# A fused attention and squared-ReLU kernel: row statistics, one v load and one k and q load at other places

## The chip, the cores and the metric

The kernel runs on one core of one Trainium2 chip. A core has five engines that run side by side, each through its own instructions in order: PE (TensorE, matrix products), DVE (VectorE), ACT (ScalarE), POOL (GpSimd) and SP (SyncE, which here only issues transfers). ACT issues some transfers too. All transfers are carried by 16 DMA engines. The metric is the device time of one execution in microseconds; the median of three runs of the kernel before is 487.42 us (486.31 to 488.24).

## The reference

The input x is 2048 rows of 512. It is normalised by row, and the result xn feeds two branches:

```python
x = A_x
xn = _layernorm(x, axis=-1)
s = _A_ref(xn, A_wqkv, A_wo)
g = _silu(_B_ref(xn, B_w1, B_b1, B_w2, B_b2))
return x + s * g
```

Branch A is attention with 32 heads of 16: each row looks at itself and at 7 rows before it, at distances of 2, 4, ... 14. So q, k and v come from one product with wqkv (512 x 1536), logits and sums over eight rows follow, and then a product with wo. Branch B is a layer of 1792 with the square of a ReLU: `h = xn @ w1 + b1`, `r = max(h, 0)`, `r * r @ w2 + b2`. All is in float32.

## The kernel before

**Tiles and stages.** The rows of x are 16 tiles of 128, and two tiles, a and a + 1, are a pair. In the first stage (up to about 140 us) each pair gets its row statistics, is normalised and transposed, and goes through the products for q, k and v. In the second stage PE runs, for four chunks of 512 rows, branch B ("up" into ph, "down" into pb) and the product with wo (pw), without a hole; meanwhile DVE works through the attention in eight units of 256 rows. Each float32 operand is split into a high and a low part, and a product takes three passes (high x high, high x low, low x high).

**The way of a tile in the first stage.** From tile 8 on, `spread(t)` computes the statistics: two ACT instructions that read all of x and keep only a sum (their output is a tile called waste), and then three small POOL operations. `norm(t)` writes the normalised tile into xn on ACT. `shuffle(t)`, for both tiles of a pair, has SP send xn to xb in four pieces, and then has it load the x tiles two pairs ahead. DVE transposes xb into PSUM (pxT); ACT copies it to xt, the high part. For a pair "of seven" (4 to 14) the products are done on sums and differences of quarters of x: DVE forms them (Sf), ACT makes their high parts and DVE their low parts. Both parts are called S, in two halves: S_0 feeds the products T1 and T2, S_1 feeds T3 and K1.

**The products of a pair of seven**, in PE's order, for pairs 6 to 12: Q0, T1, V0 and one on vsum; T2, vsum; Q1, V1; T3, vsum; K1, V1; T4, vsum. Those called pm are 512 wide, those called pv 256 wide, six matmuls each. In the profile Q0, Q1 and T4 read `pm<-wq,xt`, and T1, T2, T3 and K1 read `pm<-wq,S`. Three PSUM tiles hold them, and ACT must copy one out before PE adds to it again:
- Q0 leaves a sum that ACT copies to a second tile (`pm<-pm`, line 805) before T2 goes on in the first (line 815).
- T3's result is copied to q's staging tile (`stg<-pm`, in `sixth`, line 830) before T4 goes on in the same PSUM tile (line 864).

The staging tiles stg have four buffers, three of which a pair uses, so q's staging tile of a pair is the v staging tile of the pair before, and ACT can write it only when that one's store to sv has landed. `store_qkv` has SP store a pair's k, v and q to sk, sv and sq.

**What sets the order.** Every instruction is recorded in the order in which the Python code calls it (which is why most lines of the profile read L90, the recording helper, and L103 for SP's transfers). The pairs are written out in `pair_of_seven`, which after each of its products calls `beside(a, step)`, step 0 to 5. `beside` runs what the table `plan` holds for that place; the table is filled by `at(a, step, ...)` and, for the statistics, by `slots`. `ahead` says at which places `next_w` splits the next pair of w1 and w2 slices for branch B: two ACT instructions (`w<-w1r`, `w<-w2r`) and two on POOL. Last, `beside` calls `pump`, which fills the DVE with pieces of the attention by a clock of estimated costs. The attention asks for a unit's k, q and v with `load`, which waits until the unit's rows are stored and then defers the transfer to a due time; it is issued on ACT (`load_u`), at the first `pump` after that time. The buffers of k, q and v are one each, so a load also waits for the unit before.

Of the kernel before, what the change touches and what calls it, by code (L numbers as in the profile page):

```python
# [1 line left out]

# [52 lines left out]
BEHIND, FAR, FREE, LAND, LOAD = 5000, 9000, 2000, 4500, 10500  # L55
# [3 lines left out]
def body(ctx: ExitStack, tc: tile.TileContext, x, wqkv, wo, w1, b1, w2, b2, out):  # L59
# [3 lines left out]
    clock = {"PE": 0.0, "V": 0.0}  # L63
# [153 lines left out]
    def windows(t, i0, dims):  # L217

        part = t[:, i0]
        return bass.AP(tensor=part.tensor, offset=part.offset, ap=[part.ap[0], *dims])  # L220


    done_tiles = {n: [0, {}] for n in "qkv"}
    done_units = [0]

    def load_u(what, u):
        n = BI if what == "q" else WIN
        src = dict(q=sq, k=sk, v=sv)[what]

        t = att.tile([P, n, CH], F32, name=f"{what}{u}", tag="k" if (what, u) == ("v", NU - 1) else what)  # L230
        row = src[0, u * UP:u * UP + 1, :]
        ap = bass.AP(tensor=row.tensor, offset=row.offset, ap=[[BI * CH, NB], [src.shape[1] * CH, GR], [1, n * CH]])
        A.dma_start(t.rearrange("p i c -> p (i c)"), ap)
        return t
# [5 lines left out]
    def defer(t, f):  # L240
        behind.append((t, f))
        behind.sort(key=lambda b: b[0])

    def flush(t):
        while behind and (t is None or behind[0][0] <= t):
            behind.pop(0)[1]()

    def attention():

        tiles, Ls, landing, exps = {}, {}, {}, set()

        def qk(u, s):
            i0 = 4 * s
            yield from there("k", u)
            yield from there("q", u)
            q, k, L = tiles["q", u], tiles["k", u], Ls[u]
            yield 2350
            pr = att.tile([P, W, 2 * P], F32, name=f"pr{u}_{s}", tag="pr")  # L260
            qv = q[:, i0:i0 + 4, :].rearrange("p i c -> p (i c)")[:, None, :].to_broadcast([P, W, 2 * P])
            V.tensor_mul(pr, windows(k, i0, [[DIL * CH, W], [1, 4 * CH]]), qv)
            yield 2300
            V.tensor_reduce(
                out=L[:, s * 16:(s + 1) * 16, :].rearrange("p m w -> p w m"),
                in_=pr.rearrange("p w (g d) -> p w g d", d=HD), axis=AX.X, op=OP.add)

        def there(n, u):
            while (n, u) not in tiles:
                yield None  # L270
            not_before(landing[n, u])


        def part(u, h):
            n = BI * 4 // 2
            return slice(0, 2 * n) if h is None else slice(h * n, h * n + n)

        def soft_a(u, h=None):
            yield 1500 if h is not None else 700
            m = part(u, h)  # L280
            L, n = Ls[u][:, m], m.stop - m.start
            if u == 0:
                i = slice(m.start // 4, m.stop // 4)
                lm = L.rearrange("p (i h) w -> p i h w", h=4)
                V.tensor_add(lm, lm, mask[:, i, None, :].to_broadcast([P, n // 4, 4, W]))
            mx = att.tile([P, n], F32, name=f"mx{u}_{h}", tag="mx")
            V.tensor_reduce(out=mx, in_=L, axis=AX.X, op=OP.max)
            (G if h is None else V).tensor_sub(L, L, mx[:, :, None].to_broadcast([P, n, W]))

            def exp():  # L290
                A.activation(L, L, AF.Exp, scale=0.25)
                exps.add((u, h))

            defer(clock["V"] + (BEHIND if h is not None else FAR), exp)

        def soft_b(u, h=None):
            while (u, h) not in exps:
                yield None
            yield 2100 if h is not None else 1400
            m = part(u, h)  # L300
            L, n = Ls[u][:, m], m.stop - m.start
            sm = att.tile([P, n], F32, name=f"sm{u}_{h}", tag="sm")
            V.tensor_reduce(out=sm, in_=L, axis=AX.X, op=OP.add)
            V.reciprocal(sm, sm)
            (G if h is None else V).tensor_mul(L, L, sm[:, :, None].to_broadcast([P, n, W]))

        def av(u, s):
            i0 = 4 * s
            yield from there("v", u)
            v, L = tiles["v", u], Ls[u]  # L310
            yield 2400

            pr = att.tile([P, W // 2, 2 * P, 2], F32, name=f"pv{u}_{s}", tag="pr")
            vv = windows(v, i0, [[2 * DIL * CH, W // 2], [DIL * CH, 2], [HD, 16], [1, HD]])
            l = L[:, s * 16:(s + 1) * 16, :].rearrange("p m (a e) -> p a e m", e=2)
            V.tensor_mul(pr.rearrange("p a (g d) e -> p a e g d", d=HD), vv,
                         l[:, :, :, :, None].to_broadcast([P, W // 2, 2, 16, HD]))
            yield 2300
            V.tensor_reduce(
                out=v[:, i0:i0 + 4, :].rearrange("p i c -> p (i c)"), in_=pr.rearrange("p w n e -> p n w e"),  # L320
                axis=AX.XY, op=OP.add)

        def store(u):
            v = tiles.pop(("v", u))
            row = so[0, u * UP:u * UP + 1, :]
            dst = bass.AP(tensor=row.tensor, offset=row.offset, ap=[[BI * CH, NB], [S * CH, GR], [1, BI * CH]])
            dma(dst, v[:, :BI, :].rearrange("p i c -> p (i c)"))
            done_units[0] = u + 1

        def load(u, names):  # L330
            if u == NU:
                return
            for n in names:
                while done_tiles[n][0] < 2 * (u + 1):
                    yield None

                def start(n=n):
                    tiles[n, u] = load_u(n, u)
                    landing[n, u] = clock["PE"] + LOAD

                defer(max(clock["V"] + FREE if u else 0, done_tiles[n][1][u] + LAND), start)

        yield from load(0, "kq")

        for u in range(NU + 1):
            if u < NU:
                Ls[u] = att.tile([P, BI * 4, W], F32, name=f"L{u}", tag="L", bufs=2)
                for s in range(4):
                    yield from qk(u, s)
                    if u == 0 and s % 2:  # L350
                        yield from soft_a(0, s // 2)
                    if u == 0 and s == 1:
                        while not v_ready:
                            yield None
                        yield from load(0, "v")
                if u:
                    yield from soft_a(u)
                yield from load(u + 1, "kq")
                if u == NU - 1:
                    yield from load(u, "v")  # L360
            if u == 0:
                yield from soft_b(0, 0)
            for s in range(4):
                if u > 1 or (u == 0 and s < 2) or (u == 1 and s >= 2):
                    yield from av(max(u - 1, 0), s)
            if u == 0:
                yield from soft_b(0, 1)
            if u:
                store(u - 1)
                if u < NU - 1:  # L370
                    yield from load(u, "v")
                if u < NU:
                    yield from soft_b(u)

    v_ready = []
    stream = attention()
    coming = [None]

# [345 lines left out]
    plan = {}  # L724

    def at(a, step, f, *args):
        if args[0] < NT:
            plan.setdefault((a, step), []).append((f, args))

    for a in range(2, NT, 2):  # L730
        n, t = {2: 2, 4: 1}.get(a, 0), a + 2
# [6 lines left out]
        if seven:  # L738
# [5 lines left out]
            at(a, n + 2 if n == 2 else n + 3 if n else n + 4, low_sums, t, 0)  # L744
            at(a, n + 3 if n else n + 5, low_sums, t, 1)
    slots = {6: ((2, 2), (2, 2), (2, 2), (2, 3)), 8: ((2, 4), (2, 5), (4, 0), (4, 1)),
             10: ((4, 5), (6, 0), (6, 1), (6, 2)), 12: ((6, 3), (6, 4), (6, 5), (8, 0)),
             14: ((8, 1), (8, 2), (8, 4), (8, 5))}
    for t, places in slots.items():
        for i, (a, step) in enumerate(places):  # L750
            at(a, step, norm if i > 1 else stats if t < STATS else spread, t + i % 2)
# [6 lines left out]
        at(a, step, f, n)  # L758
    for i in range(2):
        at(4, i, load_w, i)  # L760

    ahead = {(12, 3): 1, (12, 5): 1, (14, 0): 1, (14, 2): 1, (14, 4): 1}

    def beside(a, step):

        for f, args in plan.get((a, step), ()):
            f(*args)
        for n in range(ahead.get((a, step), 0)):
            next_w()
        if (a, step) == (4, 3):  # L770
            v_ready.append(True)
        pump(LATE)

    def pair(a):
# [185 lines left out]
    for c in range(NCH):  # L960
# [82 lines left out]
        else:  # L1043
# [13 lines left out]
            for j in range(2, TPC):  # L1057
                n = D // 2 if j == TPC - 1 else D
# [25 lines left out]
```

## Time and profile before

| what | value |
|---|---|
| median of three runs | 487.42 us |
| profiled execution, its own time | 487.94 us |
| its span, first to last instruction | 486.1 us |
| PE busy | 478.4 us, 98% |
| DVE busy | 422.6 us, 87% |
| ACT busy | 240.6 us, 49% |
| POOL busy | 224.8 us, 46% |
| granted TensorE clock | 1.00 throughout |

A row of the timeline has the start in us from the span's start, the time from the first start to the last end, the engine, the code line, the operation, the tile written and the tiles read, the shapes, the number of instructions, and in brackets the idle time of the engine ahead of it with what ended it. The matmuls overlap: one that is listed as 389 ns on average starts much sooner than that after the one before it. So a wait of PE shorter than this overlap is not seen as idle time, but as a longer distance between two starts. A row of a transfer in the chain has its start and how long it took to land. In the table of windows the columns are the stretch, its length, busy time and instructions of the five kinds, the granted clock, the busy share of the DMA engines and GB/s.

### The profile page before, as it was taken

To read this page: it belongs to the slowest core of one execution; us is meant where nothing else is said; L and a number is where in the kernel's file an instruction comes from. 1 tells how busy PE (TensorE), PEld (TensorE's weight loads), DVE (VectorE), ACT (ScalarE), POOL (GpSimd) and SP (SyncE) were. 2 spreads that over 40 slices of the span, in tenths; PEclk is the share of its full clock that TensorE was granted. 3 is DMA by queue.
4 is the path that set the end of the run, shared out by engine and by line. 5 is a ranking of instruction groups with operands and counts; after the bars stand their busy time and mean duration, and the time that the engine had idled before them with its cause. 6 is when DMAs were issued, how large, how long until landed. Compare 5 with 4: busy or idle time off the path is not lost.

```text
span 486.1 us, 6125 instructions
## 1 busy us (share of the span) xinstructions
PE 478.4 (98%) x2190; PEld 396.6 (82%) x2190; DVE 422.6 (87%) x352; ACT 240.6 (49%) x441; POOL 224.8 (46%) x178
## 2 busy tenths in 40 slices
PE   8999999999999999999999999999999999999996
PEld 5887888788888888888888888888888888888885
DVE  5968995989779899999999999999999999979133
ACT  5548798747475566264512444343234543423240
POOL 1358853215787599526543332443522335252210
PEclk9999999999999999999999999999999999999999
DMA  8899999997969997471618448181617734220322
GB/s 293 235 256 236 270 285 287 224 255 231 290 167 244 260 224 178 173 163 50 169 44 211 91 145 211 19 212 43 169 43 172 232 61 133 50 90 27 86 103 72
DMA packets 71002, 81.47 MB, mean 168 GB/s; under 512 B 6204, under 2 KB 55612, under 8 KB 70972
## 3 DMA queue, kind: packets, MB, share of 16 engines
q1 hardware_dynamic: 65788, 54.87, 40.8%
q10 hardware_dynamic: 5184, 26.22, 22.3%
q8 instruction: 17, 0.28, 0.2%
q14 instruction: 13, 0.11, 0.1%
HBM read 50.60 MB, written 27.32 MB: 160 GB/s over the span
## 4 chain that ended last, share of the span: by engine, by line
PE 78%; DMA 8%; DVE 6%; POOL 3%; ACT 2%; issue 2%; SPq 1%; ACTq 0%; DVEq 0%; POOLq 0%
PE pb L90 31%; PE ph L90 31%; PE pw L90 9%; DMA xb<-xn 4%; PE pq L90 4%; DMA x<-in_A_x 2%; PE pm L90 2%; DMA k<-sk 2%; POOL vsum L90 1%; DVE L L90 1%; POOL rs L90 1%; ACT stg L90 1%; ACT waste L90 1%; SPq L103 1%; DVE xt L90 1%
## 5 line engine op out<-in xcount | busy, mean ns | idle before, releaser
L90 PE MATMUL pb<-w,h 128*128 128x512 f32 x672 | 160.1, 389 | 0.0
L90 PEld LDWEIGHTS pb<-w,h 128*128 128x128 f32 x672 | 126.2, 188 | 26.1
L90 POOL TENSOR_TENSOR h<-hf,h 128x512 fp32r<-128x512 f32 x46 | 67.6, 1470 | 157.8 <-ACT hf L90 157.8
L90 PE MATMUL ph<-xU,w 128*128 128x512 f32 x504 | 120.2, 389 | 0.0
L90 ACT ACTIVATE ph<-ph,b1t 128x512 f32<-128x512 f32 x56 | 37.0, 661 | 154.6 <-PE ph L90 144.8
L90 PEld LDWEIGHTS ph<-xU,w 128*128 128x128 f32 x504 | 94.6, 188 | 19.6
L90 DVE TENSOR_TENSOR pr<-k,q 128x2048 f32<-128x2048 f32 x32 | 79.2, 2474 | 3.0 <-DMA q<-sq 2.3
L90 DVE TENSOR_TENSOR pv<-v,L 128x2048 f32<-128x2048 f32 x32 | 77.3, 2416 | 3.8 <-POOL L L90 3.1
L90 DVE TENSOR_REDUCE v<-pv 128x256 f32<-128x2048 f32 x32 | 73.0, 2280 | 0.7
L90 DVE TENSOR_REDUCE L<-pr 128x128 f32<-128x2048 f32 x32 | 73.0, 2281 | 0.7
L90 PE MATMUL pw<-wot,oT 128*128 128x512 f32 (+1 forms) x204 | 45.9, 376 | 0.0
L90 PEld LDWEIGHTS pw<-wot,oT 128*128 128x128 f32 x204 | 36.8, 188 | 7.1
L90 PE MATMUL ph<-xT,w 128*128 128x512 f32 x168 | 40.0, 389 | 0.0
L90 PE MATMUL pm<-wq,S 128*128 128x512 f32 x144 | 37.5, 395 | 1.1 <-ACT pm L90 0.5
L90 PEld LDWEIGHTS ph<-xT,w 128*128 128x128 f32 x168 | 31.5, 188 | 6.5
L90 ACT ACTIVATE h<-ph 128x512 fp32r<-128x512 f32 x56 | 33.7, 602 | 1.8
L90 POOL TENSOR_TENSOR w<-w1r,w 128x512 fp32r<-128x512 f32 x14 | 28.4, 2031 | 12.4 <-ACT w L90 9.6
L90 PEld LDWEIGHTS pm<-wq,S 128*128 128x128 f32 x144 | 25.9, 188 | 7.3 <-DVE S L90 1.9
L90 PE MATMUL pq<-wq,xT 128*128 128x512 f32 x132 | 30.8, 392 | 0.0
L90 PEld LDWEIGHTS pq<-wq,xT 128*128 128x128 f32 x132 | 24.5, 188 | 5.8 <-ACT xT L90 0.7
L90 PE MATMUL pm<-wq,xt 128*128 128x512 f32 x108 | 27.7, 393 | 0.8 <-ACT stg L90 0.8
L90 ACT ACTIVATE hf<-ph 128x512 f32<-128x512 f32 x46 | 27.3, 594 | 0.9 <-POOL h L90 0.9
(96 smaller groups left out, 533.4 us busy)
## 6 DMA issues: line engine op xcount, KB each, us to landing
k<-sk ACTq DMA_DIRECT2D x8, 960.0 KB, 7.2
v<-sv ACTq DMA_DIRECT2D x8, 960.0 KB, 7.6
sx<-xt SPq DMA_DIRECT2D x12, 512.0 KB, 5.9
xU<-sx ACTq DMA_DIRECT2D x12, 512.0 KB, 6.1
x<-in_A_x SPq DMA_DIRECT2D x16, 256.0 KB, 6.9
sk<-stg SPq DMA_DIRECT2D x8, 512.0 KB, 4.4
sq<-stg SPq DMA_DIRECT2D x8, 512.0 KB, 6.8
sv<-stg SPq DMA_DIRECT2D x8, 512.0 KB, 5.1
```

What stands on the lines that cost most here:

```text
L90: return tc.keep_in_program_order(f(*a, **k))
L103: tc.keep_in_program_order(dma(out, in_))
```

## The change

Five things are changed, all in the first stage. PE's and DVE's instructions stay the same and in the same order.

1. Statistics of tiles 10, 12 to 15: `spread` of tile 10 at pair 4's step 4 instead of 5; of tile 13 at (6, 3), with tile 12's, instead of (6, 4); of tiles 14 and 15 both at (8, 3) instead of (8, 1) and (8, 2).
2. The first unit's v was loaded when the rows were there and pair 4's step 3 was past. It is now loaded at (8, 1), from the table.
3. The second unit's k and q are no longer deferred to a due time alone: they are held until the table releases them, k at (10, 2) and q at (10, 4), behind the blocks xb of tiles 14 and 15.
4. The first w slices are split at (12, 2) instead of (12, 3), the second at (14, 0) instead of (12, 5), the third at (14, 1) instead of (14, 0); the fourth and fifth stay.
5. By that some POOL operations and one SP store trade places: POOL's adds of pair 8's k and v come ahead of the small operations of tiles 14 and 15.

```diff
+    tiles, landing, held, released = {}, {}, {}, set()
+
+    def release(n):
+        released.add(n)
+        if n in held:
+            held.pop(n)()
+
+    def start(n, u):
+        tiles[n, u] = load_u(n, u)
+        landing[n, u] = clock["PE"] + LOAD
...
             for n in names:
                 while done_tiles[n][0] < 2 * (u + 1):
                     yield None
-
-                def start(n=n):
-                    tiles[n, u] = load_u(n, u)
-                    landing[n, u] = clock["PE"] + LOAD
-
-                defer(max(clock["V"] + FREE if u else 0, done_tiles[n][1][u] + LAND), start)
+                t = max(clock["V"] + FREE if u else 0, done_tiles[n][1][u] + LAND)
+                if u == 1 and n != "v" and n not in released:
+                    held[n] = partial(start, n, u)
+                else:
+                    defer(t, partial(start, n, u))
...
-                    if u == 0 and s == 1:
-                        while not v_ready:
-                            yield None
-                        yield from load(0, "v")
...
-             10: ((4, 5), (6, 0), (6, 1), (6, 2)), 12: ((6, 3), (6, 4), (6, 5), (8, 0)),
-             14: ((8, 1), (8, 2), (8, 4), (8, 5))}
+             10: ((4, 4), (6, 0), (6, 1), (6, 2)), 12: ((6, 3), (6, 3), (6, 5), (8, 0)),
+             14: ((8, 3), (8, 3), (8, 4), (8, 5))}
...
-
-    ahead = {(12, 3): 1, (12, 5): 1, (14, 0): 1, (14, 2): 1, (14, 4): 1}
+    at(8, 1, lambda u: start("v", u), 0)
+    plan.setdefault((10, 2), []).append((release, "k"))
+    plan.setdefault((10, 4), []).append((release, "q"))
+
+    ahead = {(12, 2): 1, (14, 0): 1, (14, 1): 1, (14, 2): 1, (14, 4): 1}
...
-        if (a, step) == (4, 3):
-            v_ready.append(True)
```

ACT at the end of pair 4 and the start of pair 6, before (the two waste rows are the statistics of tile 10; stg_0 is pair 4's last copy to q, pm_1 the copy of Q0's sum that T2 of pair 6 needs):

```order
L90 ACTIVATE S_1_697<-Sf_651 128x512
L90 ACTIVATE stg_0_570<-pm_0_571 128x8x64
L90 ACTIVATE waste_713,mean_710<-x_496 128x512
L90 ACTIVATE waste_713,rs_711<-x_496,mean_710 128x512
L90 ACTIVATE pm_1_725<-pm_0_724 128x512
```

and after:

```order
L91 ACTIVATE S_1_697<-Sf_651 128x512
L91 ACTIVATE waste_704,mean_701<-x_496 128x512
L91 ACTIVATE waste_704,rs_702<-x_496,mean_701 128x512
L91 ACTIVATE stg_0_570<-pm_0_571 128x8x64
L91 ACTIVATE pm_1_725<-pm_0_724 128x512
```

The statistics of tile 10 moved ahead of pair 4's last copy to q.

ACT in pair 8, before, from the copy Sf to the high part S_0 (x_823 and x_825 are tiles 14 and 15; `stg_0<-pm_0` is T3's result on its way to q):

```order
L90 ACTIVATE Sf_976<-pxT_950 128x256
L90 ACTIVATE waste_981,mean_978<-x_823 128x512
L90 ACTIVATE waste_981,rs_979<-x_823,mean_978 128x512
L90 ACTIVATE stg_2_911<-pv_0_917 128x4x64
L90 ACTIVATE stg_0_912<-pm_1_914 128x8x64
L90 ACTIVATE stg_2_911<-pv_2_918 128x4x64
L90 ACTIVATE stg_2_911<-pv_1_916 128x4x64
L90 ACTIVATE waste_1009,mean_1006<-x_825 128x512
L90 ACTIVATE waste_1009,rs_1007<-x_825,mean_1006 128x512
L90 ACTIVATE stg_0_912<-pm_0_913 128x8x64
L90 ACTIVATE stg_2_911<-pv_0_917 128x4x64
L90 ACTIVATE S_0_1031<-Sf_976 128x512
```

and after:

```order
L91 ACTIVATE Sf_974<-pxT_948 128x256
L91 DMA v_976<-sv 128x1x1920
L91 ACTIVATE stg_2_909<-pv_0_915 128x4x64
L91 ACTIVATE stg_0_910<-pm_1_912 128x8x64
L91 ACTIVATE stg_2_909<-pv_2_916 128x4x64
L91 ACTIVATE stg_2_909<-pv_1_914 128x4x64
L91 ACTIVATE stg_0_910<-pm_0_911 128x8x64
L91 ACTIVATE stg_2_909<-pv_0_915 128x4x64
L91 ACTIVATE S_0_1013<-Sf_974 128x512
L91 ACTIVATE waste_1020,mean_1017<-x_823 128x512
L91 ACTIVATE waste_1020,rs_1018<-x_823,mean_1017 128x512
L91 ACTIVATE waste_1029,mean_1026<-x_825 128x512
```

The statistics went behind T3's copy and S_0, and the v load, which stood in pair 6 ahead of its copy of T3, came in behind Sf.

ACT in pair 12, before (w1r_593 and w2r_594 are the first slices of branch B's weights; the last row of each piece is S_1):

```order
L90 ACTIVATE stg_2_1235<-pv_1_1240 128x4x64
L90 ACTIVATE stg_0_1236<-pm_0_1237 128x8x64
L90 ACTIVATE stg_2_1235<-pv_0_1241 128x4x64
L90 ACTIVATE S_0_1336<-Sf_1294 128x512
L90 ACTIVATE w_1340<-w1r_593 128x512
L90 ACTIVATE w_1340<-w2r_594 128x512
L90 ACTIVATE S_1_1367<-Sf_1294 128x512
```

and after:

```order
L91 ACTIVATE stg_2_1235<-pv_1_1240 128x4x64
L91 ACTIVATE w_1320<-w1r_593 128x512
L91 ACTIVATE w_1320<-w2r_594 128x512
L91 ACTIVATE stg_0_1236<-pm_0_1237 128x8x64
L91 ACTIVATE stg_2_1235<-pv_0_1241 128x4x64
L91 ACTIVATE S_0_1345<-Sf_1294 128x512
L91 ACTIVATE S_1_1367<-Sf_1294 128x512
```

The two w instructions moved ahead of the copy of T3's result that T4 of pair 12 needs.

More of the change, by code (lines that the diff above doesn't have):

```diff
@@ L1 @@
 from contextlib import ExitStack
+from functools import partial
 import concourse.bass as bass
@@ L246, in flush @@
             behind.pop(0)[1]()
+    tiles, landing, held, released = {}, {}, {}, set()
[6 more added lines that the diff above has]
+        landing[n, u] = clock["PE"] + LOAD
     def attention():
-        tiles, Ls, landing, exps = {}, {}, {}, set()
+        Ls, exps = {}, set()
         def qk(u, s):
@@ L373, in attention @@
                     yield from soft_b(u)
-    v_ready = []
     stream = attention()
```

## The prediction

> **What bounds the kernel now.** I read the first part of the page, then TensorE's (PE's) rows in the timeline, then for each hole in PE the rows of the engine that released it, and last the chain and the DMA queues.
>
> ```profile
> span 486.1 us, 6125 instructions
> ...
> PE 478.4 (98%) x2190; PEld 396.6 (82%) x2190; DVE 422.6 (87%) x352; ACT 240.6 (49%) x441; POOL 224.8 (46%) x178
> ```
>
> PE is busy for 98% of the span, and the change neither adds nor removes a matmul nor changes the order of PE or DVE. So it can gain only what PE loses to waiting, and lose only by a new wait of PE. Busy time understates waiting, since rows overlap; what counts is the distance from start to start.
>
> ```profile
> 60.50 0.88 PE L90 MATMUL pv<-vsum,S 128*128 128x256 f32 x6
> 61.86 1.65 PE L90 MATMUL pm<-wq,S 128*128 128x512 f32 x6 [0.48 <-ACT pm L90]
> ...
> 84.36 0.87 PE L90 MATMUL pv<-wq,S 128*128 128x256 f32 x6
> 86.07 1.65 PE L90 MATMUL pm<-wq,xt 128*128 128x512 f32 x6 [0.84 <-ACT stg L90]
> ...
> 89.66 1.95 PE L90 MATMUL pm<-wq,S 128*128 128x512 f32 x6
> ...
> 104.76 1.52 PE L90 MATMUL pm<-wq,S 128*128 128x512 f32 x6
> 106.12 0.88 PE L90 MATMUL pv<-wq,xt 128*128 128x256 f32 x6
> ...
> 115.24 0.88 PE L90 MATMUL pv<-wq,S 128*128 128x256 f32 x6
> 115.95 1.55 PE L90 MATMUL pm<-wq,xt 128*128 128x512 f32 x6
> ...
> 119.44 0.61 PE L90 MATMUL pm<-wq,S 128*128 128x512 f32 x2
> 120.41 1.20 PE L90 MATMUL pm<-wq,S 128*128 128x512 f32 x4 [0.36 <-DVE S L90]
> 121.45 2.90 PE L90 MATMUL pq<-wq,xt 128*128 128x512 f32 x12
> ```
>
> Undisturbed, six matmuls 512 wide take 106.12 - 104.76 = 1.36 us to the next start, and six 256 wide take 115.95 - 115.24 = 0.71. By that measure four places lose time. (1) T2 of pair 6 starts at 61.86 instead of 61.21: 0.65, and its group is 1.65 long instead of 1.55: 0.75 in all. (2) T4 of pair 8 at 86.07 instead of 85.07: 1.00 + 0.10 = 1.10. (3) T1 of pair 10 is 1.95 long instead of 1.52: 0.43. (4) T1 of pair 14 takes 121.45 - 119.44 = 2.01 instead of 1.36: 0.65. Together 2.93 us, 0.6% of the span, all where the change works. This is the ceiling.
>
> **The change, part by part.** First the statistics.
>
> ```profile
> 59.27 0.60 ACT L90 ACTIVATE stg<-pm 128x512 f32<-128x512 f32 x1 [1.12 <-POOL stg L90]
> 59.76 0.62 ACT L90 ACTIVATE waste<-x 128x512 f32<-128x512 f32 x1
> ...
> 61.23 0.58 ACT L90 ACTIVATE pm<-pm 128x512 f32<-128x512 f32 x1
> ...
> 82.93 0.60 ACT L90 ACTIVATE stg<-pm 128x512 f32<-128x512 f32 x1 [0.91 <-DMA sv<-stg]
> ...
> 83.95 0.64 ACT L90 ACTIVATE waste<-x 128x512 f32<-128x512 f32 x1
> ...
> 85.44 0.58 ACT L90 ACTIVATE stg<-pm 128x512 f32<-128x512 f32 x1
> ```
>
> Hole 1: PE waits for the copy pm<-pm, which ends at 61.81; ahead of it ACT spent 59.76 to 61.23, 1.47 us, on tile 10's statistics. At (4, 4) these stand ahead of the copy at 59.27, for which ACT sat idle 1.12 us until POOL was done. So they fill that idle time, everything behind them moves up by about 1.1, and pm<-pm ends near 60.7, before PE wants it at 61.21. Gain 0.75; price nothing, because the idle 1.12 covers most of them and PE's margin of 0.5 the rest.
>
> Hole 2: T4 of pair 8 continues the sum that T3 left in the same PSUM tile and waits for its copy to q (85.44 to 86.02). That copy stood behind tile 15's statistics (83.95 to 85.44, 1.49), and these behind a copy that waited until 82.93 for pair 6's v store. Now both tiles' statistics come at (8, 3), behind the copy, which moves up by 1.49 at least, to 84.5, ahead of 85.07. Gain 1.10. Tiles 12 to 15 now have their statistics two and two ahead of the copy S_1: 1.5 us in which only DVE's second S waits.
>
> Then v.
>
> ```profile
> 78.07 1.32 DVE L90 STREAM_TRANSPOSE pxT<-xb 128x512 f32<-128x512 f32 x2 [4.83 <-DMA xb<-xn]
> ...
> 89.68 1.28 DVE L90 TENSOR_TENSOR S<-Sf,S 128x512 fp32r<-128x512 f32 x2
> ...
> 92.13 1.31 DVE L90 STREAM_TRANSPOSE pxT<-xb 128x512 f32<-128x512 f32 x2
> ...
> 102.72 1.28 DVE L90 TENSOR_TENSOR S<-Sf,S 128x512 fp32r<-128x512 f32 x2
> 106.28 1.32 DVE L90 STREAM_TRANSPOSE pxT<-xb 128x512 f32<-128x512 f32 x2 [2.27 <-DMA xb<-xn]
> ...
> 115.36 2.58 DVE L90 TENSOR_TENSOR pr<-k,q 128x2048 f32<-128x2048 f32 x1
> ...
> 119.40 2.66 DVE L90 TENSOR_TENSOR S<-Sf,S 128x512 fp32r<-128x512 f32 x2
> ```
>
> ```profile
> 66.54 0.53 ACTq L90 DMA_DIRECT2D v<-sv  x1
> ...
> 94.67 0.52 ACTq L90 DMA_DIRECT2D k<-sk  x1
> ```
>
> ```profile
> v<-sv ACTq DMA_DIRECT2D x8, 960.0 KB, 7.6
> ```
>
> ```profile
> 71.01 6.94 DMA xb<-xn
> ...
> 95.16 11.09 DMA xb<-xn
> ```
>
> ```profile
> q10 hardware_dynamic: 98, 0.75, 103.2%
> q1 hardware_dynamic: 26, 0.01, 2.3%
> ```
>
> The last two rows are the DMA queues from 69 to 72 us: ACT's queue (q10), with v, moved 0.75 MB, SP's queue (q1), with the xb blocks of tiles 10 and 11, 0.01. So v, issued at 66.54, held the blocks back (its 960 KB take 3.9 us at that rate); they landed at 71.01 + 6.94 = 77.95, and DVE, free since 78.07 - 4.83 = 73.24, waited. Without v in front they land by about 74, and the transposes start near 74 (DVE must also wait for S_1, delayed as above). That is 4 us earlier. DVE runs in order, so the S of pair 10 (89.68) comes by 86, PE wants it at 89.66 - 1.85 = 87.8: hole 3 goes, 0.43.
>
> At (8, 1) v is issued near 79 and holds SP's queue back by up to the same 3.9 us; there now stand pair 8's stores of xt and the blocks of tiles 12 and 13. DVE will want these 4 us before 92.13, at 88.1. When they land no row of before shows. Between 88.1 (v costs them nothing) and 92.1 (all 3.9), the S of pair 12, whose first half is ready at 102.72 + 0.64 = 103.4 now, comes between 99.4 and 103.4; PE will want it at 104.76 - 2.28 = 102.5. So the price lies between 0 and 0.9 us; I take 90.5 for the landing, since part of SP's queue is emptied before v starts, and charge 0.1. Behind the v issue on ACT stand four copies of pair 8; the buffer is free since the issue at 66.54 of before, so I cost that wait at nothing.
>
> Then k and q. The fourth piece of the blocks of tiles 14 and 15 took 11.09 us to 106.25, since k, issued at 94.67, and q right behind it went first. k now goes at (10, 2), behind the last piece; the transposes at 106.28 are then bound by DVE's own order, some 3 to 4 us earlier. S of pair 14 (119.40) comes near 116, PE wants it at 119.44 - 2.3 = 117.1: hole 4 goes, 0.65. DVE's first use of k and q (115.36, then near 111.5) lies some 11 us behind q's issue near 100 (an estimate from the place of S_1 of pair 12 on ACT).
>
> What is late next is pair 12:
>
> ```profile
> 112.77 0.60 ACT L90 ACTIVATE stg<-pm 128x512 f32<-128x512 f32 x1 [1.12 <-DMA sv<-stg]
> ...
> 113.80 0.62 ACT L90 ACTIVATE stg<-pm 128x512 f32<-128x512 f32 x1
> ...
> 115.22 0.61 ACT L90 ACTIVATE w<-w1r 128x512 fp32r<-128x512 f32 x1
> 115.74 0.62 ACT L90 ACTIVATE w<-w2r 128x512 fp32r<-128x512 f32 x1
> ```
>
> ```profile
> 88.00:90.00 2.00, 2.00 (x12) 1.60 (x10) 2.00 (x5) 1.83 (x5) 0.67 (x1) 1.00 0.16 37
> ```
>
> ACT's copies of pair 12 begin when pair 10's v store has landed, at 112.7. The copy T4 needs ends at 114.42, 1.53 ahead of T4 at 115.95. The change puts the two high halves of the first w (2 x 0.52 = 1.04, by the starts 115.22 and 115.74) ahead of that copy, so T4 can start 1.72 + 1.04, about 2.75 us, after that landing. With 2.28 gained by then, PE wants T4 at 113.67, so the store would have to land by 110.9, 1.8 earlier than now. The DMA engines carry the same bytes. Their rest in that stretch is 88 to 90 (a share of 0.16 in the last row, so 1.7 us); it is used in future, but I allow 0.7 (an estimate) for a rest that opens up near 75, between the blocks without v and pair 6's stores. I let the store land 1.1 earlier, at 111.6: T4 at 114.4, a new wait of 0.7 us. Bounds: no rest opens up, 110.9, no wait; all of it opens up, 112.7, T4 at 115.45, 1.8 lost.
>
> The halves of the other w move by a step or less on ACT and are read by up products behind most of pair 14, which cover them. The three small operations of each tile's statistics on POOL move along; the adds of pair 8 now come ahead of those of tiles 14 and 15, when POOL has nothing else, so I cost them at nothing too. Sum: 0.75 + 1.10 + 0.43 + 0.65 - 0.1 - 0.7 = 2.1 us; span 484.0. The rest of the program follows PE, and the slack at the end is large:
>
> ```profile
> 459.41 0.73 DVE L90 STREAM_TRANSPOSE pT<-oq 128x512 f32<-128x512 f32 x1 [8.26 <-ACT hf L90]
> ```
>
> DVE, full until 450, then idles 8 us. The profiled execution took 487.94 (485.8 with the gain), 0.52 above the median of 487.42 (485.3). I take 485.6.
>
> [...]
>
> **The rivals.** A measurement of this kernel tells about 0.5% (2.4 us) from no change.
> - All four holes close and pair 12 does not wait. The store must land by 110.9, 1.8 earlier than now. Against it: that needs all of the 1.7 us of rest, and 1.04 us of w work is put into a margin of 1.53. For it: k and q might leave SP's queue a share. 2.9 us gained: 484.5 from the median, 485.0 from the profiled execution; chance 0.17. [...]
> - The gain is eaten in pair 12: pair 10's v store lands no earlier than now, or up to 2 us later, as more DMA work is crowded behind 79. T4 then starts at 115.45 to 117.45, 0.5 earlier to 1.5 later than now, and hole 4 gives 0.65: 486.3 to 488.3; chance 0.20.
> - Slower: v's DMA time is not absorbed but pushes pair 10's v store back. v's 3.9 us put that landing at 116.6, T4 starts at 119.35 instead of 115.95, and with hole 4 closed 2.75 us are lost: 490.2. It decides from a landing of 116.3 on. Against it: the same bytes stood before that store already. Chance 0.08.
>
> **How the numbers follow.** My forecast, with its own range of 484.8 to 486.4, has 0.55. The range 484.3 to 488.3 takes in the second rival and most of the first; outside lie the slow one and what errors in my holes add to it. Faster by over 0.5% is below 484.98: most of the first rival and a tenth of the forecast, 0.23. Slower 0.08, same 0.69.
>
> **What would show it.** PE's rows: T2 of pair 6 follows without idle time; T4 of pair 8 and T1 of pairs 10 and 14 run at the normal distance. DVE's transposes of tile 10 start near 74, of tile 14 near 102. A wait on ACT's copy before T4 of pair 12, of 0.7 us. The forecast is wrong if that wait exceeds 2 us, if S of pair 12 is waited for longer than 0.5, or if holes 1 and 2 stay.

## The result, and the profile after

Side by side on one chip, 22 runs of each: before 488.15 us in the median (486.26 to 490.82), after 485.51 (484.89 to 488.36). The ratio, which goes by the means of these runs, is 0.9958 with a 95% interval of 0.9942 to 0.9975: a gain of 0.42% or 2.03 us, between 1.2 and 2.8, about the 0.5% that the prediction took as its bound. By the medians the gain is 2.64 us. The span of the profiled execution went from 486.1 to 483.1. The first part of the page after:

```profile
span 483.1 us, 6128 instructions
...
PE 477.4 (99%) x2190; PEld 396.6 (82%) x2190; DVE 423.0 (88%) x352; ACT 240.0 (50%) x441; POOL 225.3 (47%) x178
```

PE's rows after, at the four holes and at T4 of pair 12, each with the group ahead of it:

```profile
60.55 0.88 PE L91 MATMUL pv<-vsum,S 128*128 128x256 f32 x6
61.26 1.55 PE L91 MATMUL pm<-wq,S 128*128 128x512 f32 x6
...
83.63 0.88 PE L91 MATMUL pv<-wq,S 128*128 128x256 f32 x6
84.34 1.55 PE L91 MATMUL pm<-wq,xt 128*128 128x512 f32 x6
...
87.83 1.52 PE L91 MATMUL pm<-wq,S 128*128 128x512 f32 x6
...
112.99 0.88 PE L91 MATMUL pv<-wq,S 128*128 128x256 f32 x6
113.70 1.55 PE L91 MATMUL pm<-wq,xt 128*128 128x512 f32 x6
...
117.19 1.52 PE L91 MATMUL pm<-wq,S 128*128 128x512 f32 x6
118.55 2.88 PE L91 MATMUL pq<-wq,xt 128*128 128x512 f32 x12
```

Every distance is the undisturbed one: 0.71 into T2 of pair 6 (61.26) and T4 of pair 8 (84.34), 1.52 for T1 of pair 10, 1.36 for T1 of pair 14. All four holes are closed. T4 of pair 12, where the prediction put a new wait of 0.7 us, follows after 0.71 too.

ACT's rows after, at the end of pair 4, in pair 8 and in pair 12:

```profile
57.79 0.62 ACT L91 ACTIVATE waste<-x 128x512 f32<-128x512 f32 x1
...
59.25 0.58 ACT L91 ACTIVATE stg<-pm 128x512 f32<-128x512 f32 x1
59.73 0.59 ACT L91 ACTIVATE pm<-pm 128x512 f32<-128x512 f32 x1
...
79.68 0.60 ACT L91 ACTIVATE stg<-pm 128x512 f32<-128x512 f32 x1
...
81.73 0.60 ACT L91 ACTIVATE stg<-pm 128x512 f32<-128x512 f32 x1 [0.90 <-PE pm L91]
...
109.26 0.60 ACT L91 ACTIVATE stg<-pm 128x512 f32<-128x512 f32 x1 [0.24 <-DMA sv<-stg]
...
111.33 0.61 ACT L91 ACTIVATE stg<-pm 128x512 f32<-128x512 f32 x1
```

Tile 10's statistics fill the time in which ACT waited 1.12 us for POOL before. In pair 8 the copy at 79.68 no longer waits for pair 6's v store (0.91 before), and the copy that T4 needs comes at 81.73, as soon as PE has made the sum, 2.0 us ahead of T4. In pair 12 the copies wait only 0.24 us for pair 10's v store, which has landed by 109.26, not 112.77; T4's copy ends at 111.94, 1.76 ahead of T4.

DVE's transposes of tiles 10, 12 and 14:

```profile
73.37 1.32 DVE L91 STREAM_TRANSPOSE pxT<-xb 128x512 f32<-128x512 f32 x2 [0.18 <-DMA xb<-xn]
...
89.37 1.32 DVE L91 STREAM_TRANSPOSE pxT<-xb 128x512 f32<-128x512 f32 x2 [0.47 <-DMA xb<-xn]
...
101.53 1.31 DVE L91 STREAM_TRANSPOSE pxT<-xb 128x512 f32<-128x512 f32 x2
```

The waits of 4.83 and 2.27 us for blocks (tiles 10 and 14) are down to 0.18 and none.

**The account.** For every matmul I took the distance to the next start, less the median for its shape (0.227 us for 512 wide, 0.120 for 256), and summed what is above 0.06, from 25 us on. In all 14 profiles of this study the span is this sum plus 482.6 to 483.1 us, so the holes account for the spans to half a microsecond. Before: 0.75 + 1.11 + 0.41 + 0.63 at the four places and 0.44 near 44 us. After: 0.29 near 59 us, at the S of pair 6. The last two take each other's place from profile to profile (a kernel has one or the other, v alone has both; 0.1 to 0.8 near 44 and 0.3 to 0.5 near 59), and belong to no part of the change: up to 57 us all kernels issue the same instructions in the same order.

### The profile page after: what moved, and what is told of

It reads as the page before. It is cut to its first block, busy times and chain, and to the rows that moved or that the text cites. A ratio compares the mean times of both kernels' runs of the same rounds, so it can differ in the third digit from the quotient of the medians.

```text
span 483.1 us, 6128 instructions
## 1 busy us (share of the span) xinstructions
PE 477.4 (99%) x2190; PEld 396.6 (82%) x2190; DVE 423.0 (88%) x352; ACT 240.0 (50%) x441; POOL 225.3 (47%) x178
## 4 chain that ended last, share of the span: by engine, by line
PE 98%; DMA 1%; DVE 0%; POOL 0%; issue 0%; ACT 0%; POOLq 0%
PE ph L91 32%; PE pb L91 32%; PE pm L91 12%; PE pq L91 9%; PE pw L91 9%; PE pv L91 4%; DMA x<-in_A_x 1%; PE pxT L91 0%; DVE z L91 0%; DVE st L91 0%; POOL rs L91 0%; DVE xn L91 0%; ACT xT0f L91 0%; DVE mv L91 0%; DVE rs L91 0%
## 5 line engine op out<-in xcount | busy, mean ns | idle before, releaser
L91 POOL TENSOR_TENSOR w<-w1r,w 128x512 fp32r<-128x512 f32 x14 | 31.6, 2259 | 23.4 <-ACT w L91 23.2
```

The lines of the kernel that those rows point to most:

```text
L91: return tc.keep_in_program_order(f(*a, **k))
```

## The experiments

Two theories stood against each other at first. **H**: each hole belongs to the part of the change that was written beside it, so parts add up. **C**: the holes from pair 8 on hang on one chain of transfers (blocks of x, v, stores, k and q). In the table each kernel has its median, its ratio to before with the interval, the span of its profile, and PE's holes by place, in us:

| kernel | median | ratio to before | span | T2 p6 | pair 8 | T1 p10 | T4 p12 | T1 p14 | after 126 | 43 to 60 |
|---|---|---|---|---|---|---|---|---|---|---|
| before | 488.15 | 1 | 486.1 | 0.75 | 1.11 | 0.41 | 0 | 0.63 | 0 | 0.44 |
| after | 485.51 | 0.9958 [0.9942, 0.9975] | 483.1 | 0 | 0 | 0 | 0 | 0 | 0 | 0.29 |
| statistics back | 486.06 | 0.9958 [0.9933, 0.9983] | 483.8 | 0 | 0 | 0 | 0 | 0.70 | 0 | 0.30 |
| v back | 487.19 | 0.9982 [0.9958, 1.0005] | 485.2 | 0 | 0.49 | 1.70 | 0 | 0 | 0 | 0.33 |
| k, q back | 486.26 | 0.9991 [0.9964, 1.0017] | 484.1 | 0 | 0 | 0 | 0 | 1.11 | 0 | 0.33 |
| w back | 485.69 | 0.9955 [0.9932, 0.9978] | 483.1 | 0 | 0 | 0 | 0 | 0 | 0 | 0.41 |
| statistics alone | 490.13 | 1.0035 [1.0009, 1.0060] | 488.6 | 0 | 0 | 1.62 | 0 | 2.12 | 1.45 | 0.29 |
| v alone | 489.69 | 1.0016 [0.9988, 1.0044] | 487.7 | 0 | 0 | 0 | 0 | 4.09 | 0 | 0.85 |
| k, q alone | 487.27 | 0.9978 [0.9952, 1.0004] | 485.8 | 0.75 | 1.53 | 0 | 0 | 0 | 0 | 0.82 |
| 4 copies late | 486.44 | 0.9962 [0.9938, 0.9987] | 484.2 | 0 | 0 | 0 | 0.69 | 0 | 0 | 0.43 |
| 6 copies late | 489.02 | 1.0008 [0.9977, 1.0039] | 486.4 | 0 | 0 | 0 | 2.01 | 0 | 1.55 | 0.12 |
| 7 copies late | 490.03 | 1.0039 [1.0011, 1.0067] | 488.9 | 0 | 0 | 0 | 3.04 and 1.51 | 0 | 1.04 | 0.39 |
| v also stored | 487.60 | 0.9991 [0.9962, 1.0021] | 484.9 | 0 | 0 | 0 | 0.30 | 1.50 | 0 | 0.11 |
| xT also stored | 486.35 | 0.9963 [0.9941, 0.9984] | 486.0 | 0 | 0 | 0 | 0.23 | 0 | 2.46 | 0.47 |

The 1.51 of seven copies, and some 1.7 of the 4.09 of v alone, are matmuls at half the clock (last section). The medians come from five sets of runs, each with its own runs of before (488.15 us beside after; 488.4 for the next seven kernels and seven copies, 488.9 for four and six copies and v also stored, 487.9 for xT also stored), and single runs of one kernel scatter by 3 us and more; where a few tenths matter I go by the holes.

### One part undone at a time

**Statistics back.** The slots as before, all else as after:

```diff
-             10: ((4, 4), (6, 0), (6, 1), (6, 2)), 12: ((6, 3), (6, 3), (6, 5), (8, 0)),
-             14: ((8, 3), (8, 3), (8, 4), (8, 5))}
+             10: ((4, 5), (6, 0), (6, 1), (6, 2)), 12: ((6, 3), (6, 4), (6, 5), (8, 0)),
+             14: ((8, 1), (8, 2), (8, 4), (8, 5))}
```

> The changed kernel with the statistics of tiles 10 and 12 to 15 back at their old steps. Theory H (each hole of PE belongs to the part that I costed it with): holes 1 and 2 come back, 0.75 + 1.10 us, so 1.85 us slower than the changed kernel, about 0.8 us faster than before. Theory C (the holes from pair 8 on hang on one chain of transfers, and statistics are only one of two causes of hole 2): hole 1 comes back with 0.75; hole 2 stays closed, because pair 6's v store, for which ACT waited until 82.93 before, lands near 79 once v is out of its way. So 0.75 slower than the changed kernel, about 1.9 us faster than before.

Holes 1 and 2 stay closed: 0.70 lost at one place only, T1 of pair 14. ACT, PE and DVE of this kernel:

```profile
58.07 0.60 ACT L91 ACTIVATE stg<-pm 128x512 f32<-128x512 f32 x1 [0.34 <-POOL stg L91]
...
83.34 0.58 ACT L91 ACTIVATE stg<-pm 128x512 f32<-128x512 f32 x1
```

```profile
84.18 1.55 PE L91 MATMUL pm<-wq,xt 128*128 128x512 f32 x6
...
118.08 1.20 PE L91 MATMUL pm<-wq,S 128*128 128x512 f32 x4 [0.43 <-DVE S L91]
```

```profile
91.00 1.32 DVE L91 STREAM_TRANSPOSE pxT<-xb 128x512 f32<-128x512 f32 x2 [2.19 <-DMA xb<-xn]
...
116.52 2.64 DVE L91 TENSOR_TENSOR S<-Sf,S 128x512 fp32r<-128x512 f32 x2
```

Hole 2: with v moved, pair 6's v store lands early enough that nothing in pair 8 waits, and the copy ends at 83.92 even behind the statistics, 0.26 ahead of T4. Hole 1: ACT waits 0.34 for POOL instead of 1.12, since POOL's add took 1.29 us here and 1.78 in the profile of before. With the old slots the add took 1.78 in two profiles (before; k, q alone), which have hole 1, and 1.29 in two (this one; v alone), which have not. With the new slots it took 1.79 to 1.84 in four, without a hole. So the new slot protects against a slow add; that it is worth 0.75 in each run isn't shown: in the profile of after the add took 1.29 too, so hole 1 need not have been there with the old slot either. The length of the add goes with who starts first. In the six profiles with 1.78 to 1.84, DVE's S starts 0.01 to 0.05 us ahead of it (before: 57.40 and 57.45); in the eight with 1.28 to 1.31 it starts 0.01 to 0.23 behind (after: 57.14 and 56.91). These six are also the profiles whose small hole lies near 44 us alone, where no part of the change is at work yet. So whether an execution has hole 1 is in part a matter of its kind, and one profile of each kernel doesn't tell how often each kind comes. What is lost here is a thing that I had not listed: with the statistics of tile 14 ahead of v's issue on ACT, v leaves at 79.87 instead of 77.74, the transposes of tile 12 start at 91.00 instead of 89.37, and DVE, without a wait for the next 25.5 us, hands that on to the S of pair 14.

**v back.** v is loaded from the stream once pair 4's step 3 is past, as before, and the line at (8, 1) goes:

```diff
+                    if u == 0 and s == 1:
+                        while not v_ready:
+                            yield None
+                        yield from load(0, "v")
...
-    at(8, 1, lambda u: start("v", u), 0)
```

> The changed kernel with the first unit's v loaded where it was before. Theory H: only hole 3 comes back, 0.43 us, so 2.2 us faster than before. Theory C: the blocks of tiles 10 and 11 land late again (about 76.7, their issue being 1.3 earlier than before), PE is 1.85 earlier by then, so T1 of pair 10 waits about 1.0 us, more than the 0.43 of before, and T1 of pair 12 may wait up to 0.5; 1.3 to 1.8 us faster than before.

```profile
88.78 0.70 PE L91 MATMUL pm<-wq,S 128*128 128x512 f32 x2 [0.45 <-ACT waste L91]
90.22 1.20 PE L91 MATMUL pm<-wq,S 128*128 128x512 f32 x4 [0.73 <-DVE S L91]
```

T1 of pair 10 loses 1.70, not 0.43: the blocks of tile 10 are as late as before (DVE transposes them at 77.87, before 78.07), and since PE is 1.4 earlier by then (T4 of pair 8 at 84.69, not 86.07), it waits the longer. The first of the two rows names the statistics (`waste`) as what ended the wait, but those end at 88.78, behind the first weight load of T1 at 88.75, and the copy of S_0 was done at 85.72, ahead of them. What ended just before is an add of DVE, late with its transposes:

```profile
87.96 0.68 DVE L91 TENSOR_TENSOR stg<-stg,pm 128x512 f32<-128x512 f32 x1
```

Another 0.49 is lost in pair 8 (81.78), behind a copy of ACT that waited 1.25 us for pair 6's k store. By spans v's move is worth 2.1 us, more than any other part.

**k and q back.** The hold and both releases go:

```diff
-                if u == 1 and n != "v" and n not in released:
+                if False:
...
-    plan.setdefault((10, 2), []).append((release, "k"))
-    plan.setdefault((10, 4), []).append((release, "q"))
```

> The changed kernel with the second unit's k and q sent as soon as they are due, at pair 10's step 1. Theory H: hole 4 comes back with 0.65 us; 2.0 us faster than before. Theory C: if the last piece of the blocks of tiles 14 and 15 is overtaken by k and q as before (landing near 105), the S of pair 14 is as late as before, and since PE comes 2.3 us earlier the hole grows to about 2 us; 0.6 us faster than before. If the pieces are all sent before k (the last at 93.0 in the changed kernel, k near 94), no hole and no loss: the hold would then be worth nothing.

```profile
104.15 1.32 DVE L91 STREAM_TRANSPOSE pxT<-xb 128x512 f32<-128x512 f32 x2 [2.69 <-DMA xb<-xn]
```

k overtakes the last blocks of tile 14 again, DVE waits 2.69 us for them, and T1 of pair 14 loses 1.11, more than the 0.63 of before for the same reason: PE arrives earlier.

**w back.** `ahead` as before:

```diff
-    ahead = {(12, 2): 1, (14, 0): 1, (14, 1): 1, (14, 2): 1, (14, 4): 1}
+    ahead = {(12, 3): 1, (12, 5): 1, (14, 0): 1, (14, 2): 1, (14, 4): 1}
```

> The changed kernel with the w1 and w2 slices split at their old steps. In its profile the copy before T4 of pair 12 ended at 111.94 and T4 began at 113.70, so the w halves ahead of it (1.05 us) lie in a margin of 1.76 and taking them away gains nothing: the same time as the changed kernel within 0.3 us, 2.6 us faster than before. If the prediction's wait in pair 12 (0.7 us) does occur in most executions, this kernel is 0.7 us faster than the changed one.

Nothing changes: span 483.1, median 485.69. Moving the w work ahead of T4's copy neither costs nor gains.

### One part alone

The parts are those of the three diffs above, each put into the kernel before on its own, with `ahead` as before.

**Statistics alone.**

> The kernel before with the new steps of the statistics alone. Theory H: holes 1 and 2 close, 1.85 us faster than before. Theory C: hole 1 closes, hole 2 nearly (v still delays pair 6's v store), but the S of pairs 10 and 14 hang on transfers that come only some 1.3 us earlier, by the earlier normalisation of tile 11; so hole 3 grows from 0.43 to about 1.0 and hole 4 stays near 0.65 to 1.2: 1.0 to 1.3 us faster than before.

Neither theory holds: this part alone makes the kernel slower than before, 1.0035 [1.0009, 1.0060]. DVE and PE:

```profile
77.37 1.32 DVE L91 STREAM_TRANSPOSE pxT<-xb 128x512 f32<-128x512 f32 x2 [4.23 <-DMA xb<-xn]
...
106.76 1.32 DVE L91 STREAM_TRANSPOSE pxT<-xb 128x512 f32<-128x512 f32 x2 [3.45 <-DMA xb<-xn]
```

```profile
88.29 0.70 PE L91 MATMUL pm<-wq,S 128*128 128x512 f32 x2 [0.35 <-ACT waste L91]
89.72 1.19 PE L91 MATMUL pm<-wq,S 128*128 128x512 f32 x4 [0.73 <-DVE S L91]
...
121.22 1.21 PE L91 MATMUL pm<-wq,S 128*128 128x512 f32 x4 [1.54 <-DVE S L91]
```

Holes 1 and 2 close, as H says: PE is 1.8 us earlier at pair 8. But the blocks of tile 10 land where they did (DVE at 77.37, before 78.07), and those of tile 14 too (106.76, before 106.28), because v and k still stand before them. So PE waits there for what it won (at 88.29 too for DVE's add, which ended at 88.14, and not for the statistics): 1.62 at pair 10 and 2.12 at pair 14, where its second half starts at 121.22, not at 120.41; why the blocks of tile 14 land half a microsecond later than before is open. Another 1.45 is lost after 160 us (last section).

**v alone.**

> The kernel before with the first unit's v loaded at (8, 1) alone. Theory H: hole 3 closes, 0.43 us faster; holes 1, 2 and 4 stay. Theory C: holes 2 and 3 close (1.10 + 0.43), hole 1 stays with 0.75, and hole 4 grows by as much as PE is ahead less what the blocks of tiles 14 and 15 gain: about 1.0 instead of 0.65. So 1.2 us faster than before, with hole 2 closed although tile 15's statistics stand where they stood.

```profile
118.25 0.70 PE L91 MATMUL pm<-wq,S 128*128 128x512 f32 x2 [0.45 <-DVE stg L91]
120.47 2.05 PE L91 MATMUL pm<-wq,S 128*128 128x512 f32 x4 [1.52 <-DVE S L91]
122.32 3.69 PE L91 MATMUL pq<-wq,xt 128*128 128x512 f32 x12
```

With v's move alone holes 2 and 3 are closed, as C says. Hole 1 is gone too, but by POOL's quick add (above). All of this is given back in pair 14, which k and q still bind: T1's second half starts at 120.47, where it started before (120.41). (With the new slots too, k and q back above, it starts at 118.48: there the blocks of tile 14 leave SP from 89.39 on, not 91.70, and k, at 92.26 against 93.10, overtakes fewer.) It even costs more, since PE then ran at half its clock (0.51, last section).

**k and q alone.**

> The kernel before with the second unit's k and q held alone. Both theories: hole 4 closes, 0.65 us faster; holes 1, 2 and 3 stay as before. DVE's transposes of tile 14 at 104.0, without a wait, instead of 106.28.

Hole 4 closes, and hole 3 with it, since hole 2 (1.53 here) makes PE so late that the S of pair 10 is in time. Measured 1.1 us by medians, 0.9978 [0.9952, 1.0004], 0.3 by spans.

What follows from the seven: the holes are not terms of a sum but dates. Blocks held back by v set one date for PE in pair 10 (T1's second part at 89.72 and 90.22 where v is as before), blocks held back by k and q another in pair 14 (120.41, 121.22 and 120.47 before, with the statistics alone and with v alone). Closing a hole ahead of a date that stays moves the loss behind it. Only with all dates moved does the gain come through.

### The margin of pair 12

**Copies on ACT.** In pair 12's step 2, ahead of the w halves and of T4's copy, n copies more (n = 4, 6, 7) into tiles that nobody reads:

```diff
+    def idle_w(n):
+        for i in range(n):
+            spare = hpool.tile([P, 512], F32, name=f"spare{i}", tag="hf")
+            A.activation(spare, raws[1][1], AF.Copy)
+
+    at(12, 2, idle_w, 7)
```

> The changed kernel with seven more ACT copies of 128 x 512, whose result nobody reads, ahead of the w halves in pair 12 (7 x 0.52 = 3.64 us). The margin before T4 of pair 12 was 1.76 us, so T4 should wait 1.9 us and, if the rest of the program follows PE, the kernel take 1.9 us longer than the changed one. If less is lost, something behind pair 12 makes it up; if more, the delay also hits another wait.

> After, with four copies more on ACT in pair 12, ahead of the two halves of w (the copies go to a tile that is not read). In the profile with seven such copies they took 4.63 us, so 0.65 each: 2.6 us. The copy that T4 needs has a margin of 1.76 by after's profile, so T4 waits 0.85 us. Theory K (a wait this short leaves the granted clock at 1.00): 0.85 us lost, span 484.0, median 486.4. Theory L (any wait of PE there is followed by some 3.5 us at half the clock, as with seven copies): 0.85 and about 1.6 more, span 485.5, median 488.

> After, with six such copies more: 3.9 us, T4 waits 2.15 us. Theory K: the wait is nearly that of the kernels with one part alone (1.9 and 2.3 us lost inside 4 us), where some runs show a mean clock of 0.993 to 0.997 and others 0.999 to 1.000; so the profile may show either, and the median lies between 487.6 (wait alone) and 489.3 (with half the clock for 3.5 us). Theory L: always with half the clock, 489.3.

Seven copies:

```profile
110.43 4.63 ACT L91 ACTIVATE spare<-w2r 128x512 f32<-128x512 f32 x7
```

```profile
116.64 2.70 PE L91 MATMUL pm<-wq,xt 128*128 128x512 f32 x6 [2.74 <-ACT stg L91]
119.14 1.41 PE L91 MATMUL pv<-vsum,xt 128*128 128x256 f32 x6
```

```profile
117.00:119.00 2.00, 2.00 (x6) 1.60 (x5) 1.59 (x2) 0.89 (x2) 2.00 (x2) 0.50 0.85 246
```

Six copies, PE:

```profile
115.31 1.65 PE L91 MATMUL pm<-wq,xt 128*128 128x512 f32 x6 [1.74 <-ACT stg L91]
```

A copy took 0.65 us, not the 0.52 that I had taken for the first of these kernels, so seven are 4.6 and not 3.64. T4 loses 0.69, 2.01 and 3.04 us (0.14 of the last already at half clock): the delay less 1.6 to 1.9. So the 1.76 us of margin read from the profile is real. With six copies the median, 489.02, is near the upper end that was expected, but this profile shows the clock at full and 1.55 us lost after 160 us instead. Behind the long wait six matmuls 512 wide take 2.50 us to the next start (119.14 - 116.64) instead of 1.39: the granted clock is 0.50 in that window. With four copies T4 loses 0.69 against 0.85 expected and the matmuls behind it run undisturbed (theory K).

**One transfer more on ACT's queue,** right behind q, ahead of pair 10's v store. First 960 KB from v's tile:

```diff
     plan.setdefault((10, 4), []).append((release, "q"))
+    spare = dram.tile([P, WIN * CH], F32, name="spare")
+
+    def store_v(n):
+        A.dma_start(spare, tiles[n, 0].rearrange("p i c -> p (i c)"))
+
+    plan[10, 4].append((store_v, "v"))
```

> After, with one more transfer of 960 KB on ACT's queue right behind the second unit's q (the first unit's v is also written to a scratch array; the output does not use it). It stands ahead of pair 10's v store, which was issued at 101.79 and landed 7.37 us later. In every kernel so far that store is issued 11.9 us before T4 of pair 12, and T4 can start 2.75 after the landing, so up to 9.15 us of latency cost nothing. Theory I (the store's issue goes with PE, its latency with the bytes queued before it): v's load takes 3.9 us at its rate, so the latency rises to about 11.3, T4 waits about 2.1 us, and the span is 485.2, by the median 487.6. Theory F (the queues have room there, so the transfer is absorbed): latency under 9.15, no wait, 485.5.

```profile
108.50 2.29 DVE L91 TENSOR_REDUCE v<-pv 128x256 f32<-128x2048 f32 x1 [3.28 <-DMA spare<-v]
```

The median, 487.60, is the number of theory I, but for another reason: DVE sums into v's tile and waited 3.28 us for the copy, and that cost T1 of pair 14 1.50. T4 lost 0.30 only. So the kernel was made again with xT, a tile nobody writes then, as the source (1 MB):

```diff
+        A.dma_start(spare, xT[n][:, :2].rearrange("p k t h n -> p (k t h n)").bitcast(F32))
```

> As the other kernel with one more transfer behind q, but it copies half of xT (1 MB, no engine writes that tile again soon) instead of v, so that DVE's sum into v does not wait for it. Theory S (the two queues share the DMA engines, so the store of pair 10 is pushed back by about half of the new transfer's time, as in the other kernel, from 7.37 to about 9.3 us of latency): T4 of pair 12 waits 0.2 to 0.5 us, T1 of pair 14 does not wait, span 483.5, median 485.9. Theory I (all bytes that are issued earlier go first): latency near 11.4, T4 waits 2.2, span 485.3, median 487.7.

Its transfers from 99 to 109 us (size, median time from issue to landing), and ACT's and PE's rows:

```profile
spare<-xT ACTq DMA_DIRECT2D x1, 1024.0 KB, 9.1
...
sv<-stg SPq DMA_DIRECT2D x1, 512.0 KB, 9.2
```

```profile
111.14 0.60 ACT L91 ACTIVATE stg<-pm 128x512 f32<-128x512 f32 x1 [1.14 <-PE pm L91]
```

```profile
113.86 1.65 PE L91 MATMUL pm<-wq,xt 128*128 128x512 f32 x6
```

The store took 9.2 us instead of 7.4: 1 MB more ahead of it (4.1 us at v's rate) pushed it back by 1.8, not by 4.1. The row of ACT names PE, but the same copy waits for `sv<-stg` in after (0.24) and with v also stored (1.18), and here the store landed at 101.84 + 9.2 = 111.04. T4 starts 2.72 behind this copy (113.86 - 111.14) and loses 0.23. Theory S, that the queues share, fits, and theory I does not. (The 2.46 after 126 us of this profile I put down to the scatter of the last section; the ten spans of this kernel go from 482.8 to 486.6.)

## Why the prediction was right, and where it was wrong

The time was right: 485.6 forecast, 485.51 measured. So was the gain by the means, 2.03 us against 2.1. That the time fits to 0.1 is luck: the forecast starts from 487.42 for the kernel before, which beside after came out at 488.15, and by the medians the gain is 2.64. The account was not right: the likeliest case named a wait that did not come, and the profile shows the case that had been given 0.17, all four holes closed and no wait in pair 12, with 2.90 us in them (3.05 with the holes that come and go). Why the means show 0.9 less than the two profiles is not settled; that some executions of before have no hole 1 is likely by POOL's two lengths, but not shown, since each kernel has one profile and its runs scatter by 3 us and more.

- **The four gains** (0.75, 1.10, 0.43, 0.65; sum 2.93): by the sum over all matmuls 0.75, 1.11, 0.41, 0.63; sum 2.90. Both are read from the one profile of before; what after adds is that all four are 0 in its own. The reading was right to 0.02, and that these sizes hold in each execution isn't shown.
- **What closes them**: wrong for two. Hole 2 was put down to the statistics; v's move alone closes it, by pair 6's v store, and so do the statistics alone. Hole 1 too is gone with v moved and the old slots, but there because POOL's add was quicker. My reading of the rows was of what stood directly ahead of the late copy; I didn't ask why the copy ahead of that had waited for a store.
- **S of pair 12** (−0.1): measured 0. The blocks of tile 12 landed for 89.37, against 90.5 taken. By the prediction's own rows a landing at 90.5 would have cost nothing either: S at 103.4 - (92.1 - 90.5) = 101.8, and PE wants it at 102.5.
- **T4 of pair 12** (−0.7): this is the step that failed; measured 0. The prediction let pair 10's v store land at 111.6, 1.1 earlier than before, as if full DMA engines fixed the landing while PE gains 2.28. It was in by 109.26. A row of SP (its issue) and one of the transfers (size, time from issue to landing) show why, first before, then after:

```profile
104.05 2.58 SPq L103 DMA_DIRECT2D sv<-stg  x1
```

```profile
sv<-stg SPq DMA_DIRECT2D x1, 512.0 KB, 8.6
```

```profile
101.79 0.36 SPq L104 DMA_DIRECT2D sv<-stg  x1
```

```profile
sv<-stg SPq DMA_DIRECT2D x1, 512.0 KB, 7.4
```

  The issue moved by 2.26, which is all that PE gained: in 13 of the 14 profiles (all but v alone) the store is issued 11.8 to 11.9 us ahead of the undisturbed start of T4 (before: 115.95 - 104.05 = 11.90; after: 113.70 - 101.79 = 11.91). The latency fell by 1.2 on top. So the right form of the term is a latency: T4 waits if the store takes longer than 11.9 - 2.75 = 9.15 us, and it took 7.4; even with 1 MB more it took 9.2.
- **The DMA engines' rest**: I allowed 0.7 for a new rest. The windows from 66 us to the landing, before and after:

```profile
66.00:112.67 46.67, 45.69 (x259) 39.62 (x259) 39.02 (x52) 33.97 (x78) 13.21 (x19) 1.00 1.05 266
```

```profile
66.00:109.16 43.16, 43.16 (x249) 37.92 (x248) 40.33 (x54) 32.59 (x74) 12.12 (x18) 1.00 1.05 276
```

  266 GB/s in 46.67 us are 12.4 MB, 276 in 43.16 are 11.9. So 0.5 MB less moved between 66 us and the landing (some 0.4 of it had gone before 66, since pair 4 ended earlier), and the rest went faster: about 1.9 and 1.6 us of the 3.5. My sum held the bytes fixed.
- **The first rival** (k and q might leave SP's queue a share, a landing by 110.9, 2.9 us; 0.17) came out closer than my forecast. In after from 98 to 101, with k and q under way, SP's queue moved 0.34 MB beside 0.63 of ACT's. I had read the rows of before from 69 to 72 (0.75 MB against 0.01) as one queue holding the other back. The queue rows of after from 82 to 84, while v is loaded beside blocks:

```profile
q10 hardware_dynamic: 63, 0.48, 90.0%
q1 hardware_dynamic: 63, 0.06, 13.3%
```

  As many packets from each queue, 63, but 8 times the bytes for v's. So bytes alone, by which I had read the rows, don't show that one queue holds the other back. The packets are not equal everywhere, though: the rows of 69 to 72 have 98 against 26, those of after from 98 to 101 have 82 against 346, and before, from 69.5 to 72 and from 98 to 101, SP's queue moved no packet (ACT's 84 and 85), though blocks issued from 69.07 on, and one at 95.16, were still on their way. What decides is open.
- **The slower rival** (v's 3.9 us push the store back to 116.6; 0.08): the last experiment prices it. 1 MB more pushed the store by 1.8, not by its whole time, and T4 lost 0.23.

## What to carry to other kernels

Holes of one engine in a row are dates, not terms: before adding gains, ask of every later hole what sets its date, and expect a part of the change on its own to move the loss rather than to remove it (statistics alone, +0.35%). A store that frees a buffer should be costed as issue plus latency, with the issue tied to the engine that makes its data, not as a landing at a fixed time (pair 10's v store: 101.79 + 7.4 in after, 104.05 + 8.6 before). If two causes stand in a row before a late instruction, undo each by itself before you name one.

## What the runs showed of the hardware

**Behind waits of 1.97 and 2.74 us PE ran at half its clock for 3.4 us.** With seven copies T4 waited 2.74 us, and from about 116.9 to 120.3 the matmuls ran at a clock of 0.50. In the profile of v alone, after waits of 0.45 and 1.52 inside 4 us, the clock was at half from about 120.5 to 123.9, and the window of 121 to 124 shows it at 0.51:

```profile
121.00:124.00 3.00, 3.00 (x8) 2.32 (x7) 3.00 (x2) 1.44 (x3) 2.49 (x3) 0.51 1.02 271
```

With six copies (1.74 us of wait) and with the statistics alone (1.54) the profile stays at 1.00, but of the twelve runs of statistics alone four have a mean clock of 0.995 or 0.996, of v alone seven have 0.993 to 0.997, and of the ten with six copies two have 0.996 and 0.997; in their 22 runs each, before and after never fell below 0.998. 3.4 us at half the clock cost 1.7 us and lower the mean by 0.0035 (1.7 of 486). So in these profiles the clock fell after 1.97 (in two pieces) and 2.74 us of idle time, but not in every run: three of the twelve with seven copies show 1.000. What else decides whether it falls is not shown.

**The next date is 40 us on.** Where PE lost time after 160 us, DVE had waited for the third unit's q, here with xT also stored, and then in after:

```profile
161.44 2.29 DVE L91 TENSOR_TENSOR pr<-k,q 128x2048 f32<-128x2048 f32 x1 [5.17 <-DMA q<-sq]
```

```profile
158.43 2.29 DVE L91 TENSOR_TENSOR pr<-k,q 128x2048 f32<-128x2048 f32 x1 [2.46 <-DMA q<-sq]
```

In the ten profiles with a wait of 1.1 to 2.6 PE has no hole there; with 3.4 (six copies), 4.27 (seven copies), 4.75 (statistics alone) and 5.17 it loses 1.55, 1.04, 1.45 and 2.46. That this makes the 3 us of scatter between runs of one kernel is likely, but only argued: single runs were not profiled.
